# Batch 1's first softmax five steps later, and state's read with 32-column weights and a transpose

## The chip, the core and the metric

The kernel runs on one core of a Trainium2 chip. The metric is the device time of one execution in microseconds (us); the time before is the median of three runs. The profile is of one further execution of the same program, so its times are those of that one execution.

## The reference

The program computes an attention with a learned state of 32 rows for each head (4 batches, 8 heads, 512 positions, 64 columns a head), and sends the result, 4 x 544 rows of 512, through two feed-forward layers with 2048 inner columns. Cut to what matters here:

```python
scores  = scale * x @ state.T                  # B, H, 512, 32
a       = softmax(scores)                      # "first softmax", over the 32 state rows
xread   = a @ state                            # 512 rows a head
scores2 = scale * state @ x.T                  # B, H, 32, 512
a2      = softmax(scores2)                     # "second softmax", over the 512 positions
sread   = a2 @ x                               # "state's read", 32 rows a head
x1 = concat([xread, sread])                    # 544 rows a batch
h  = x1 @ w_in ;  g = h - tanh(h) ;  x2 = g @ w_out
h  = x2 @ w2_in;  g = h * tanh(softplus(h)) ;  out = g @ w2_out
```

Everything is float32. The attention's own products are plain float32; a feed-forward product is made of three products of a large and a small part (names ending in h and l, type fp32r).

## The kernel before

The first feed-forward layer runs as a list of steps, `seq`: 16 steps for each batch (a step is one tile of 128 inner columns for the 512 rows of a batch), 4 steps for the state rows of all batches after batch 2, and then batch 3. Batch 0 has steps 0 to 15, batch 1 steps 16 to 31, batch 2 steps 32 to 47, the state rows 48 to 51, batch 3 steps 52 to 67. Step i issues an "up" (six products into `h`, from `ath`, `atl`, `swh`, `swl`) and then the "down" of three steps before (twelve products into `acc`, from `gh`, `gl` and the weights). Between the two stand the side jobs of that step, entered with `at(step, ...)`: reading weights in and splitting them (`conv_w1o`, names `w`, `r`, `wh`, `wl`), products of a batch's state with weights (`sw`, names `swp`, `swh`, `swl`), and the attention of the next batches. A framework then orders the instructions of each engine, each engine runs its own in that order, and semaphores tie the engines together.

For one batch the attention is: transposes of x (`xt_t`, bank `xtp`), scores (`sc_m`, bank `sct`, copied to `scs`), for each half j the first softmax (`at_exp`: transpose into bank `sc`, maximum, subtraction, exponential; `at_norm`: sum, reciprocal, product, all on tile `a`), the second softmax (`at_exp_t`, on `scs`), its transpose (`at_read_t`, bank `e2p`, copied to `e2`), and state's read (`at_sread`, bank `srd`), which goes into `xst` for steps 48 to 51. `at_a` transposes `a` (bank `atp`) into `ath` and `atl`, which the batch's "up" steps read. VectorE (DVE) does reductions and differences, ScalarE (ACT) the exponentials, tanh and half of the copies. Beyond the start, all side jobs share two PSUM banks (`side_bank`), one after the other.

In `at_sread` a product has 64 columns of x as its weights and 32 columns of the softmax as what moves, and writes 64 partitions; two of them (i = 0 and 1) write the two halves of the partitions.

The profile gives line 63 for nearly every instruction (a helper issues them), so the rows are told apart by the tiles' names; a tile in a second kind of buffer is called `wide`.

Of the kernel before, what the change touches and what calls it, by code (L numbers as in the profile page):

```python
# [75 lines left out]
def attention_moe_kernel(  # L76
# [12 lines left out]
    NS = state.shape[2]  # L89
# [3 lines left out]
    KD = DM // 128  # L93
# [10 lines left out]
    TE, AC, V = (Pinned(e, order) for e in (nc.tensor, nc.scalar, nc.vector))  # L104
# [13 lines left out]
    def get(name, dtype=F32, newest=False):  # L118
        if halves and dtype == F32:
            return halves.popleft()  # L120
        i = free.pop() if newest else free.popleft()
        return Unit(slots.tile([128, 512], dtype, tag=f"k{i}", name=name), i)

    def put(*units):
        for u in units:
            if u.slot is None:
                halves.append(u)
            else:
                free.append(u.slot)
# [4 lines left out]
    def side_bank(name):  # L134
        ps_n[0] += 1
        return psum.tile([128, 512], F32, tag=banks[ps_n[0] % len(banks)], name=name)

    ident = misc.tile([128, 128], F32, name="ident")
# [271 lines left out]
    def load_x(b, ks=range(KD)):  # L410
        for k in ks:
            u = get("x", newest=b > 1)
            (nc.gpsimd if b > 1 else nc.sync).dma_start(
                out=u.t.rearrange("p (h c) -> p h c", h=2),
                in_=x[b, 2 * k:2 * k + 2].rearrange("h (p r) d -> p h (r d)", r=4),
            )
            X[b, k] = u

    def x_tile(b, k, i, r):
        c = i * 256 + r * 64  # L420
        return X[b, k].t[:, c:c + 64]

    P = {}
# [17 lines left out]
    def at_xt(b, k):  # L441
        xt_t(b, k)
        xt_c(b, k)
# [31 lines left out]
    def at_scores(b):  # L475
        sc_m(b)
        for j in range(2):
            sc_c(b, j)

    def sc_t(b, j):  # L480
        P["s", b, j] = ps = side_bank("sc")
        for r in range(4):
            TE.transpose(
                out=ps[:, r * 128:(r + 1) * 128],
                in_=SC[b, j].t[:, r * 128:(r + 1) * 128],
                identity=ident,
            )

    def sc_max(b, j):
        P["m", b, j] = mx = small.tile([128, 16], F32, tag="mx", name="mx")  # L490
        V.tensor_reduce(out=mx, in_=v3(P["s", b, j]), axis=AX.X, op=ALU.max)

    def sc_sub(b, j):
        A[b, j] = get("a")
        V.tensor_tensor(
            out=v3(A[b, j].t),
            in0=v3(P.pop(("s", b, j))),
            in1=P.pop(("m", b, j)).unsqueeze(2).to_broadcast([128, 16, NS]),
            op=ALU.subtract,
        )  # L500

    def sc_exp(b, j):
        AC.activation(out=A[b, j].t, in_=A[b, j].t, func=ACTF.Exp, scale=scale)

    def at_exp(b, j):
        sc_t(b, j)
        sc_max(b, j)
        sc_sub(b, j)
        sc_exp(b, j)

    def nm_sum(b, j):
        P["n", b, j] = sm = small.tile([128, 16], F32, tag="sm", name="sm")
        V.tensor_reduce(out=sm, in_=v3(A[b, j].t), axis=AX.X, op=ALU.add)

    def nm_rec(b, j):
        sm = P["n", b, j]
        V.tensor_scalar(out=sm, in0=sm, scalar1=1e-9, scalar2=None, op0=ALU.add)
        V.reciprocal(out=sm, in_=sm)

    def nm_mul(b, j):  # L520
        a3 = v3(A[b, j].t)
        V.tensor_tensor(
            out=a3,
            in0=a3,
            in1=P.pop(("n", b, j)).unsqueeze(2).to_broadcast([128, 16, NS]),
            op=ALU.mult,
        )

    def at_norm(b, j):
        nm_sum(b, j)  # L530
        nm_rec(b, j)
        nm_mul(b, j)

    def at_exp_t(b, j):
        e = SC.pop((b, j))
        mt = small.tile([128, 2], F32, tag="mt", name="mt")
        V.tensor_reduce(out=mt[:, 0:1], in_=e.t, axis=AX.X, op=ALU.max)
        V.tensor_scalar(
            out=mt[:, 0:1], in0=mt[:, 0:1], scalar1=-scale, scalar2=None, op0=ALU.mult
        )  # L540
        AC.activation(
            out=e.t, in_=e.t, func=ACTF.Exp, scale=scale, bias=mt[:, 0:1], accum_out=mt[:, 1:2]
        )
        V.tensor_scalar(
            out=mt[:, 1:2], in0=mt[:, 1:2], scalar1=1e-9, scalar2=None, op0=ALU.add
        )
        V.reciprocal(out=mt[:, 1:2], in_=mt[:, 1:2])
        V.tensor_scalar(
            out=e.t, in0=e.t, scalar1=mt[:, 1:2], scalar2=None, op0=ALU.mult
        )  # L550
        ET[b, j] = e

    def at_read_t(b, j):
        ps = side_bank("e2p")
        e = ET.pop((b, j))
        for r in range(4):
            TE.transpose(
                out=ps[:, r * 128:(r + 1) * 128],
                in_=e.t[:, r * 128:(r + 1) * 128],
                identity=ident,  # L560
            )
        u = get("e2")
        AC.activation(out=u.t, in_=ps, func=ACTF.Copy)
        put(e)
        ET[b, j] = u

    def at_sread(b):
        ps = side_bank("srd")
        u = [ET.pop((b, i)) for i in range(2)]
        for k in range(KD):  # L570
            for r in range(4):
                for i in range(2):
                    c = r * 128 + k * NS
                    TE.matmul(
                        out=ps[i * 64:(i + 1) * 64, k * NS:(k + 1) * NS],
                        lhsT=x_tile(b, k, i, r),
                        rhs=u[i].t[:, c:c + NS],
                        start=(r == 0),
                        stop=(r == 3),
                    )  # L580
        put(*u, *(X.pop((b, k)) for k in range(KD)))
        V.tensor_copy(
            out=xst[:, :, b * NS:(b + 1) * NS],
            in_=ps[:, :128].rearrange("p (k n) -> p k n", k=KD),
        )

    def at_steps(b):
        st = [lambda k=k: at_xt(b, k) for k in range(KD - 1)]
        return st + [
            lambda: at_xt(b, KD - 1),  # L590
            lambda: at_scores(b),
            lambda: (at_exp(b, 0), at_exp_t(b, 0)),
            lambda: at_norm(b, 0),
            lambda: (at_exp(b, 1), at_exp_t(b, 1), at_read_t(b, 0)),
            lambda: at_norm(b, 1),
            lambda: at_read_t(b, 1),
            lambda: at_sread(b),
        ]

    def at_a_hi(b, j):  # L600
# [469 lines left out]
    def at(step, fn, back=None):  # L1070

        def held():
            kept = [e.floor for e in engines]
            for e, m in zip(engines, marks[-back]):
                e.floor = m
            fn()
            for e, m in zip(engines, kept):
                e.floor = m

        side.setdefault(step, []).append(held if back else fn)  # L1080

    seq = []
    start = {}
# [14 lines left out]
        for c in range(4):  # L1098
            at(start[b] + 4 * c - 2, lambda b=b, c=c: sw(b, c))
    for j in range(2):  # L1100
        at(7 + j, lambda j=j: at_exp(1, j))
        at(8 + j, lambda j=j: at_norm(1, j))
        for b in range(2):
            k = start[1] + 4 + 2 * b + 4 * j
            at(k, lambda b=b, j=j: at_exp_t(b, j), 1)
            at(k + 3 - b, lambda b=b, j=j: at_read_t(b, j), 1)
            if j:
                at(k + 4 - b, lambda b=b: at_sread(b), 1)
    for b in (2, 3):
        at(start[b - 1], lambda b=b: load_x(b))  # L1110
        for i, f in zip((3, 4, 5, 7, 8, 9, 10, 11, 12, 13, 15), at_steps(b), strict=True):
            at(start[b - 1] + i, f)
    for b in (1, 2, 3):
        at(start[b] - (3 if b > 1 else 1), lambda b=b: at_a(b))
# [202 lines left out]
```

## Time and profile before

| | |
|---|---|
| median of 3 runs | 717.06 us (716.99 to 717.49) |
| the profiled execution | 717.59 us |
| its span, first to last instruction | 715.8 us |
| TensorE (PE) busy | 706.3 us |
| VectorE (DVE) busy | 464.7 us |
| ScalarE (ACT) busy | 352.5 us |
| granted TensorE clock | 1.0 throughout |

The span is 1.8 us shorter than the time of the same execution. A busy TensorE is a TensorE that has something in its pipe: its instructions overlap, so the distance from one start to the next says what one costs, not its duration. A float32 product stands in the trace as two records, each with its own weight load (PEld); a transpose and an fp32r product as one.

### The profile page before, as it was taken

What the parts mean: (1) busy time and instruction counts of PE and PEld (TensorE: products, weight loads), DVE (VectorE), ACT (ScalarE), POOL (GpSimd) and SP (SyncE); (2) the same over time, 40 slices, a digit from 0 to 9 for tenths busy, and PEclk for the clock granted to TensorE, in tenths of its full rate; (3) what the DMA queues carried; (4) which work ended last, traced back from release to release, by engine and by line L of the source; (5) the groups of instructions that cost most, each with busy time, mean ns of one, the idle gap of its engine ahead of it and who ended that gap; (6) DMA issues with size and microseconds to landing.
All of it is one profiled execution on the core that took longest, in us unless ns stands there. A gap on an engine that the chain in (4) does not pass through costs nothing.

```text
span 715.8 us, 10555 instructions
## 1 busy us (share of the span) xinstructions
PE 706.3 (99%) x3974; PEld 566.4 (79%) x3974; DVE 464.7 (65%) x793; ACT 352.5 (49%) x631; POOL 70.5 (10%) x110
## 2 busy tenths in 40 slices
PE   8899999999999999999999999999999999999998
PEld 6467777778777898777878888888888888888886
DVE  5899755675758747798647875557753455545654
ACT  6998545556765656867537342224333223222320
POOL 0000010022412224420304100000000000000000
PEclk9999999999999999999999999999999999999999
DMA  9985210124644357691978654445866244322003
GB/s 288 341 278 195 60 60 1 31 89 145 215 172 147 118 177 251 220 381 45 335 269 286 230 173 153 142 150 147 292 199 213 89 163 153 126 77 85 1 1 132
DMA packets 52643, 118.66 MB, mean 166 GB/s; under 512 B 7280, under 2 KB 11632, under 8 KB 52592
## 3 DMA queue, kind: packets, MB, share of 16 engines
q1 hardware_dynamic: 44272, 90.72, 38.4%
q0 software_dynamic: 8320, 27.27, 10.5%
q8 instruction: 31, 0.51, 0.3%
q14 instruction: 20, 0.16, 0.1%
HBM read 88.34 MB, written 29.62 MB: 165 GB/s over the span
## 4 chain that ended last, share of the span: by engine, by line
PE 87%; ACT 7%; DVE 4%; issue 1%; DMA 1%; SPq 0%
PE acc L63 48%; PE h L63 32%; ACT r L63 2%; ACT w L63 2%; PE swp L63 2%; PE hs L63 2%; PE srd L63 1%; ACT gh L63 1%; DMA x<-in_x_dram 1%; DVE w L63 1%; ACT t L63 1%; DVE wide L63 1%; PE xtp L63 1%; DVE a L63 1%; PE sct L63 1%
## 5 line engine op out<-in xcount | busy, mean ns | idle before, releaser
L63 PE MATMUL acc<-wo,gh 128*128 128x512 f32 (+1 forms) x548 | 168.1, 388 | 0.0
L63 PE MATMUL h<-yh,ws 128*128 128x512 f32 x448 | 156.7, 391 | 0.1
L63 PEld LDWEIGHTS acc<-wo,gh 128*128 128x128 f32 x548 | 102.1, 188 | 21.0 <-ACT gh L63 0.4
L63 DVE TENSOR_TENSOR wide<-acc,wide 128x512 f32<-128x512 f32 (+1 forms) x99 | 67.7, 684 | 74.5 <-PE acc L63 73.2
L63 PE MATMUL acc<-wo,gl 128*128 128x512 f32 (+1 forms) x274 | 106.3, 388 | 0.0
L63 PE MATMUL acc<-gh,wh 128*128 128x512 f32 x244 | 99.1, 406 | 0.0
L63 PEld LDWEIGHTS h<-yh,ws 128*128 128x128 f32 x448 | 84.1, 188 | 17.8 <-DVE mt L63 0.5
L63 PE MATMUL acc<-gh,wl 128*128 128x512 f32 x244 | 95.6, 392 | 0.0
L63 PE MATMUL acc<-gl,wh 128*128 128x512 f32 x244 | 95.1, 390 | 0.0
L63 PE MATMUL h<-yl,ws 128*128 128x512 f32 x224 | 87.2, 389 | 0.0
L63 DVE TENSOR_TENSOR gl<-wide,gh 128x512 fp32r<-128x512 f32 x70 | 48.3, 690 | 48.1 <-ACT gh L63 48.0
L63 DVE TENSOR_TENSOR wide<-h,wide 128x512 f32<-128x512 f32 x92 | 63.2, 687 | 21.6 <-ACT wide L63 10.4
L63 ACT ACTIVATE wide<-wide 128x512 f32<-128x512 f32 x47 | 29.7, 633 | 85.4 <-DVE wide L63 85.4
L63 ACT ACTIVATE wide<-h 128x512 f32<-128x512 f32 x39 | 23.3, 596 | 75.6 <-PE h L63 74.8
L63 PEld LDWEIGHTS acc<-wo,gl 128*128 128x128 f32 x274 | 51.5, 188 | 10.9 <-DVE gl L63 0.4
L63 PEld LDWEIGHTS acc<-gh,wh 128*128 128x128 f32 x244 | 45.8, 188 | 17.2 <-issue 5.6
L63 PEld LDWEIGHTS acc<-gh,wl 128*128 128x128 f32 x244 | 45.8, 188 | 11.3 <-issue 1.2
L63 PE MATMUL h<-ath,swh 128*128 128x512 f32 x128 | 51.8, 405 | 1.8 <-DVE t L63 1.0
L63 PEld LDWEIGHTS acc<-gl,wh 128*128 128x128 f32 x244 | 45.9, 188 | 8.5
L63 DVE TENSOR_TENSOR t<-h,t 128x512 f32<-128x512 f32 x54 | 36.9, 685 | 23.5 <-ACT t L63 23.4
L63 PE MATMUL h<-ath,swl 128*128 128x512 f32 x128 | 50.5, 395 | 0.5 <-DVE swl L63 0.5
L63 PE MATMUL h<-atl,swh 128*128 128x512 f32 x128 | 50.0, 390 | 0.0
(158 smaller groups left out, 1037.4 us busy)
## 6 DMA issues: line engine op xcount, KB each, us to landing
ws<-wi SPq DMA_DIRECT2D x128, 256.0 KB, 3.8
wo<-wo SPq DMA_DIRECT2D x64, 256.0 KB, 3.8
st<-in_moe_w_in_dram SPq DMA_DIRECT2D x27, 512.0 KB, 5.6
st<-in_moe_w_out_dram SPq DMA_DIRECT2D x22, 512.0 KB, 4.8
wi<-wh POOLq DMA_DIRECT2D x32, 256.0 KB, 4.1
wi<-wl POOLq DMA_DIRECT2D x32, 256.0 KB, 4.3
wide<-in_moe_w_out_dram SPq DMA_DIRECT2D x10, 512.0 KB, 5.3
wo<-wh POOLq DMA_DIRECT2D x16, 256.0 KB, 5.0
```

What stands on the lines that cost most here:

```text
L63: i = fn(*args, **kw)
```

## The change

Three things are changed. Batch 1's first softmax (`at_exp(1, j)` and `at_norm(1, j)`) stands at steps 12 to 14 and no longer at 7 to 9. State's read takes 32 columns of the softmax as weights and 64 columns of x as what moves, in the order i, r, k, so that four successive products write the four quarters of the partitions; the result goes to a tile `sr`, and a new job `at_sturn` two or more steps later turns it with one 128x128 transpose (bank `srt`) into `xst`. And batch 3's attention, with the load of its x, stands two or three steps earlier.

```diff
     def at_sread(b):
         ps = side_bank("srd")
         u = [ET.pop((b, i)) for i in range(2)]
-        for k in range(KD):
+        for i in range(2):
             for r in range(4):
-                for i in range(2):
+                for k in range(KD):
                     c = r * 128 + k * NS
                     TE.matmul(
-                        out=ps[i * 64:(i + 1) * 64, k * NS:(k + 1) * NS],
-                        lhsT=x_tile(b, k, i, r),
-                        rhs=u[i].t[:, c:c + NS],
+                        out=ps[k * NS:(k + 1) * NS, i * 64:(i + 1) * 64],
+                        lhsT=u[i].t[:, c:c + NS],
+                        rhs=x_tile(b, k, i, r),
                         start=(r == 0),
                         stop=(r == 3),
                     )
         put(*u, *(X.pop((b, k)) for k in range(KD)))
+        P["r", b] = o = get("sr")
+        V.tensor_copy(out=o.t[:, :128], in_=ps[:, :128])
+
+    def at_sturn(b):
+        ps = side_bank("srt")
+        u = P.pop(("r", b))
+        TE.transpose(out=ps[:, :128], in_=u.t[:, :128], identity=ident)
+        put(u)
         V.tensor_copy(
             out=xst[:, :, b * NS:(b + 1) * NS],
...
-        at(7 + j, lambda j=j: at_exp(1, j))
-        at(8 + j, lambda j=j: at_norm(1, j))
+        at(12 + j, lambda j=j: at_exp(1, j))
+        at(13 + j, lambda j=j: at_norm(1, j))
...
                 at(k + 4 - b, lambda b=b: at_sread(b), 1)
+                at(k + 7 - b, lambda b=b: at_sturn(b), 1)
+    when = {2: (3, 4, 5, 7, 8, 9, 10, 11, 12, 13, 15, 16), 3: (0, 1, 3, 4, 5, 7, 8, 9, 10, 11, 12, 13)}
     for b in (2, 3):
-        at(start[b - 1], lambda b=b: load_x(b))
-        for i, f in zip((3, 4, 5, 7, 8, 9, 10, 11, 12, 13, 15), at_steps(b), strict=True):
+        at(start[b - 1] - 2 * (b - 2), lambda b=b: load_x(b))
+        for i, f in zip(when[b], at_steps(b), strict=True):
             at(start[b - 1] + i, f)
```

**VectorE, steps 7 to 9.** The order of VectorE's instructions from the second half of step 6 on (`mx`, `sm` and `a` are the first softmax's, `w`, `wl` the weights', `t`, `gl` a step's own). Before:

```order
L63 TENSOR_TENSOR wl<-w,wh 128x512
L63 SCALAR_TENSOR_TENSOR w<-w,r 128x512 x2
L63 TENSOR_REDUCE mx<-sc 128x16
L63 TENSOR_TENSOR t<-h,t 128x512
L63 TENSOR_TENSOR a<-sc,mx 128x512
L63 TENSOR_TENSOR wl<-w,wh 128x512
L63 TENSOR_TENSOR gl<-t,gh 128x512
L63 SCALAR_TENSOR_TENSOR w<-w,r 128x512
L63 TENSOR_REDUCE sm<-a 128x16
```

Now:

```order
L63 TENSOR_TENSOR wl<-w,wh 128x512
L63 SCALAR_TENSOR_TENSOR w<-w,r 128x512 x3
L63 TENSOR_TENSOR t<-h,t 128x512
L63 TENSOR_TENSOR wl<-w,wh 128x512
L63 SCALAR_TENSOR_TENSOR w<-w,r 128x512
L63 TENSOR_TENSOR gl<-t,gh 128x512
```

The softmax's instructions are gone from between the weights' and the step's own, here and in the two steps that follow.

**VectorE, steps 12 to 14.** The same engine behind the second `swl` of step 11, up to the `swl` of step 14. Before:

```order
L63 TENSOR_TENSOR wl<-w,wh 128x512 x2
L63 TENSOR_TENSOR t<-h,t 128x512
L63 TENSOR_TENSOR gl<-t,gh 128x512
L63 TENSOR_TENSOR t<-h,t 128x512
L63 TENSOR_TENSOR gl<-t,gh 128x512
L63 SCALAR_TENSOR_TENSOR w<-w,r 128x512
L63 CAST wh<-w 128x512
```

Now:

```order
L63 TENSOR_TENSOR wl<-w,wh 128x512
L63 TENSOR_REDUCE mx<-sc 128x16
L63 TENSOR_TENSOR t<-h,t 128x512
L63 TENSOR_TENSOR a<-sc,mx 128x512
L63 TENSOR_TENSOR gl<-t,gh 128x512
L63 TENSOR_REDUCE sm<-a 128x16
L63 TENSOR_SCALAR sm<-sm 128x16
L63 RECIPROCAL sm<-sm 128x16
L63 TENSOR_TENSOR a<-a,sm 128x512
L63 TENSOR_REDUCE mx<-sc 128x16
L63 TENSOR_TENSOR t<-h,t 128x512
```

The softmax's instructions, six for each half, stand here now (the last ones shown begin the second half), ahead of the `swl` of step 14 and of the transposes of `a` at step 15.

**TensorE, step 29.** The order of TensorE behind batch 1's state read (`e2p` and `atp` are transposes, `acc` the twelve products of a "down"). Before:

```order
L63 MATMUL srd<-e_1504,x 64x32
L63 MATMUL srd<-wide,x 64x32
L63 MATMUL e2p<-ident,wide 128x128 x4
L63 MATMUL acc_1307<-gh,wh 128x512
L63 MATMUL acc_1307<-gl,wh 128x512
L63 MATMUL acc_1307<-gh,wl 128x512
L63 MATMUL atp<-ident,a 128x128 x8
L63 MATMUL acc_1308<-gh,wh 128x512
```

Now:

```order
L63 MATMUL srd<-x,e_1504 32x64 x16
L63 MATMUL srd<-x,e_1762 32x64 x16
L63 MATMUL e2p<-ident,wide 128x128 x4
L63 MATMUL atp<-ident,a 128x128 x4
L63 MATMUL acc_1307<-gh,wh 128x512
L63 MATMUL acc_1307<-gl,wh 128x512
L63 MATMUL acc_1307<-gh,wl 128x512
L63 MATMUL atp<-ident,a 128x128 x4
L63 MATMUL acc_1308<-gh,wh 128x512
```

Half of the transposes of `a` stand before the three products that were ahead of all eight. The four new transposes stand in three other places: one right before batch 2's read (step 31), two side by side at step 32, one at step 45.

## Rows read from the trace of the kernel before

**Rows 1.** The page: engines' busy time; the chain that ended last, by engine.

```profile
PE 706.3 (99%) x3974; PEld 566.4 (79%) x3974; DVE 464.7 (65%) x793; ACT 352.5 (49%) x631; POOL 70.5 (10%) x110
...
PE 87%; ACT 7%; DVE 4%; issue 1%; DMA 1%; SPq 0%
```

**Rows 2.** Windows: stretch, length, then each engine's busy time, clock, DMA share, GB/s.

```profile
48.00:69.20 21.20, 21.20 (x104) 17.22 (x96) 20.61 (x39) 19.60 (x36) 0.00 (x0) 1.00 0.67 241
69.20:75.40 6.20, 5.71 (x35) 3.51 (x35) 6.20 (x12) 4.65 (x9) 0.00 (x0) 1.00 0.00 0
75.40:89.00 13.60, 13.60 (x119) 10.90 (x118) 8.75 (x14) 6.34 (x11) 0.00 (x0) 1.00 0.26 78
...
177.00:252.00 75.00, 75.00 (x460) 58.78 (x459) 53.44 (x99) 48.16 (x88) 19.99 (x30) 1.00 0.48 162
...
363.00:716.00 353.00, 349.23 (x1594) 289.83 (x1593) 204.65 (x320) 114.80 (x196) 9.12 (x14) 1.00 0.46 151
```

**Rows 3.** Timeline of PE at step 12: start, duration, idle time before and its releaser.

```profile
73.17 0.50 PE L63 MATMUL h<-ath,swh 128*128 128x512 f32 x1
...
74.39 0.50 PE L63 MATMUL h<-ath,swl 128*128 128x512 f32 x1 [0.49 <-DVE swl L63]
```

**Rows 4.** Timeline of DVE at steps 7 and 12.

```profile
53.18 0.68 DVE L63 TENSOR_REDUCE mx<-sc 128x16 f32<-128x512 f32 x1
53.78 0.68 DVE L63 TENSOR_TENSOR t<-h,t 128x512 f32<-128x512 f32 x1
...
73.66 0.68 DVE L63 TENSOR_TENSOR swl<-swp,swh 128x512 fp32r<-128x512 f32 x1
```

**Rows 5.** Timeline of PE at step 29: first, second and last pairs of batch 1's read.

```profile
160.44 0.24 PE L63 MATMUL srd<-e,x 128*64 128x32 f32 x1
...
160.52 0.22 PE L63 MATMUL srd<-e,x 128*64 128x32 f32 x1
160.53 0.22 PE L63 MATMUL srd<-wide,x 128*64 128x32 f32 x1
...
162.27 0.22 PE L63 MATMUL srd<-e,x 128*64 128x32 f32 x1
```

**Rows 6.** The chain in order of time, 153 to 176 us: start, length, what.

```profile
173.49 1.99 PE srd L63 x64
```

**Rows 7.** Timeline of PE at step 24: batch 2's scores, 256 columns on 32-column tiles.

```profile
133.48 0.38 PE L63 MATMUL sct<-wide,sbt 64*32 64x256 f32 x1
...
133.52 0.38 PE L63 MATMUL sct<-wide,sx 64*32 64x256 f32 x1
133.69 0.38 PE L63 MATMUL sct<-wide,sbt 64*32 64x256 f32 x1
```

**Rows 8.** Timeline of PE in the second layer: two transposes between products.

```profile
525.47 0.39 PE L63 MATMUL acc<-wo,gl 128*128 128x512 f32 x1
525.70 0.38 PE L63 MATMUL gt<-ident,wide 128*128 128x128 f32 x2
...
526.15 0.40 PE L63 MATMUL h<-yl,ws 128*128 128x512 f32 x1
```

**Rows 9.** Timeline of ACT at step 29.

```profile
160.55 0.60 ACT L63 ACTIVATE t<-h 128x512 f32<-128x512 f32 x1 [2.06 <-PE h L63]
...
161.90 0.63 ACT L63 ACTIVATE gh<-t 128x512 fp32r<-128x512 f32 x1
...
163.18 0.60 ACT L63 ACTIVATE wide<-e2p 128x512 f32<-128x512 f32 x1 [0.65 <-PE e2p L63]
```

**Rows 10.** Timeline of DVE at step 29.

```profile
161.18 0.69 DVE L63 TENSOR_TENSOR t<-h,t 128x512 f32<-128x512 f32 x1 [2.45 <-ACT t L63]
...
162.54 0.29 DVE L63 COPY xst<-srd 128x128 f32<-128x128 f32 x1
```

**Rows 11.** Timeline of POOL, whose queue issues stores and batch 3's x.

```profile
179.36 0.72 POOL L261 DMA_DIRECT2D wi<-wh  x1 [12.74 <-ACT wh L63]
```

**Rows 12.** Tile x, 85 to 260 us, POOL's part: last line of the answer.

```profile
DMA to landing us min/median/max: 3.1/3.3/4.3
```

More of the change, by code (lines that the diff above doesn't have):

```diff
@@ L597, in at_steps @@
             lambda: at_sread(b),
+            lambda: at_sturn(b),
         ]
```

## The prediction

> **What bounds the kernel now.** I read the page first, then windows, then timelines of the places that the change touches. The page has TensorE busy for 706.3 of 715.8 us, and the chain that ended last is TensorE's for 87% [rows 1]. So the question is which stretches leave TensorE waiting. The windows answer it [rows 2]: from 177 to 252 us, where batch 3's attention lies, it is busy for 75.00 of 75.00; after 363 us it lacks 3.8 us in 353, in the second layer and the tail, where the change has no instruction. From 48 to 69 us TensorE is full too, but VectorE is busy for 20.61 and ScalarE for 19.60 of 21.20: weights are being read in. From 69.2 to 75.4 VectorE is never idle and TensorE lacks 0.5 us. That is the one wait near the moved softmax: at step 12 the third product of the "up" starts 1.22 us after the first [rows 3], where two ordinary distances of 0.23 (525.47 to 525.70 [rows 8]) make 0.46. It is 0.76 late, and its releaser is `swl`, which VectorE began at 73.66 and held for 0.68 [rows 4]: the product starts 0.05 after it. VectorE was behind with its queue.
>
> Where TensorE is full, a microsecond taken from its instructions is one taken from the end, as long as nothing that it waits for becomes the last; where it waits for VectorE, only VectorE's work counts.
>
> **The change part by part.** The sum is made against the profiled execution, 717.59 us.
>
> *State's read.* The old read runs in pairs: i = 0 and i = 1 start 0.01 apart [rows 5], so two halves of the columns work at once. From the second pair to the last, 160.52 to 162.27, are 30 distances: 58.3 ns a pair. 32 pairs (16 products for each i, two records each) make 1.87, and with 0.12 for getting in and out that is the 1.99 of [rows 6]. The new read has the same 64 records. If its four quarters work at once, they are 16 rounds. No row shows 128 rows by 32 columns, so a round's price is bounded. From below: in the scores, on tiles of 32 columns by 64 rows, eight records start within 0.04 and the same tile starts again 0.21 later with 256 columns moving [rows 7]; 64 columns need a quarter, 53 ns. From above: weights and stream might lie one behind the other, half of 58.3 for half the weight columns and 53 for the stream, 82 ns. I take 58.3, the row of the same operation with the same 128 rows: its 128 weight columns for a pair are again 128 for a round of four. So 16 rounds go, 0.93 us a read, 3.73 for four (bounds 2.24 and 4.08). A read is then 1.05 long.
>
> The Trainium skill ("TensorE: Matmul & The Clock Gate", section on LDWEIGHTS) has a weight load take its columns over 1.2 GHz, 53 ns for 64 and 27 for 32. By that the old pair would be bound by weights and the new round by its stream, and this term 4.08; the rows here cannot separate the two, since both give the old pitch.
>
> *The turns.* Four transposes are added. Two between products push the second product behind them from 0.46 to 0.68 us after the last one ahead (525.47 to 526.15 [rows 8]): 0.22. They stand in three places. Two single ones cost between 0.11 and 0.22 each, 0.13 taken since little of it is entry; the two at step 32 cost 0.22. Together 0.48. The four extra copies on VectorE (0.29 each [rows 10]) lie beside TensorE's work: VectorE has 21 us free between 177 and 252 [rows 2].
>
> *The split of `atp` at step 29.* One more entry to transposes, 0.05 (0 to 0.1).
>
> *A new wait at step 29.* Two banks serve all side jobs. The read uses one, `e2p` the other, the first half of `atp` the first again, the second half the second. So the first half waits for VectorE's copy of `srd`, the second for ScalarE's copy of `e2p`. I count from the start of the read, 160.44 [rows 5], which I call E. ScalarE starts tanh at E + 0.11 and `gh` at E + 1.46 [rows 9]; VectorE starts `t` at E + 0.74 [rows 10], and a large instruction holds it for 0.60 (53.18 to 53.78 [rows 4]). In the new order the copy of `srd` follows `t`: E + 1.34 to 1.63. TensorE, a microsecond sooner, is through with the read and `e2p` (four transposes, 0.43) at E + 1.48: 0.15 of waiting. Behind that come four transposes and three products, to E + 2.8; but ScalarE's copy of `e2p` now stands behind `gh` and a `wh`, some 0.6 each, and is done at about E + 3.2. That is 0.4 more. 0.6 in all (0 to 1.2: nothing if ScalarE gets there sooner, double if a weight is late). Queued behind it on TensorE is the rest of the "down" and all later work, so it counts in full. Before, the copy of `e2p` started at 163.18, E + 2.74, and nothing waited.
>
> *The softmax five steps later.* VectorE loses from steps 7 to 9 eight large instructions of 0.60 and four small ones, about 5.2 us, in a stretch where it was full to the end; that is more than the 0.76 by which `swl` was late. So that wait goes: -0.76 (bound 0). The transposes `sc` cost TensorE the same in either place. The work comes back at steps 12 to 14, where VectorE is busy for 8.75 of 13.60 [rows 2], part of it the backlog that is gone by then. With 5.2 more it is nearly full, but the last product on `a` is needed only at step 15. I take no new wait, and price one below.
>
> *Batch 3 three steps earlier.* Same instructions; TensorE is full in the old place and in the new. Its x is issued at step 30 by POOL's queue and first read at step 32; a load lands 3.3 us after its issue [rows 12], and two steps of 18 products at 0.23 are 8.3. Taken as 0.
>
> The sum: -3.73 + 0.48 + 0.05 + 0.60 - 0.76 = -3.36, so 714.23 for the profiled execution. The median stands 0.53 below it (717.06), so I forecast **713.7**. What a measurement of this kernel can tell from no change is about 0.2%, 1.4 us; the forecast is beyond it.
>
> **The rivals.**
>
> *Weights do not overlap with the stream.* Rounds of 82 ns, a term of 2.24, and a wait at step 29 of 0.2 since TensorE comes later: -2.24 + 0.53 + 0.2 - 0.76 = -2.27, 714.8. For it: no row shows four quarters with all 128 rows, and 58.3 is also what half weights and half stream in series could give. Against it: in the pairs the records already lie on one another, 0.22 long and 0.058 apart. The Trainium skill (same page, Part 3, "The mechanism") says that a weight load overlaps with running matmuls only where the row group differs; here all have all rows, so by that rule this rival would hold. Chance 0.12.
>
> *The quarters do not run four abreast.* Two abreast, as now: the reads stay at 1.99, the wait at step 29 does not arise, and -0.76 + 0.53 leaves 716.8, no change. One at a time: 64 x 58.3 = 3.73 and the 0.12, so 7.5 more over four reads, 724.3. Against both: the scores run on four column quarters (and two row halves) at once [rows 7]. Chances 0.05 and 0.03.
>
> *VectorE is late at steps 12 to 15.* 8.75 + 5.2 is 13.95 in 13.60 us if the backlog is not gone in time; then `atp` at step 15 or the "up" of step 16 waits, between 1 and the 2.6 us that one half of the softmax costs VectorE: 714.7 to 716.3. It decides from the moment when the last product on `a` ends after TensorE reaches step 15. For it: VectorE runs in order, and its softmax alternates with ScalarE's exponential. Against it: from the transposes of step 13 it has two steps, 8.3 us, for four instructions of the softmax and some six of the steps' own, 6 us. Chance 0.08.
>
> *Slower: batch 3's x comes late.* POOL runs its queue in order, and the last of the four loads, which the first transpose needs, stands behind four stores of weights. Before the change a store stood for 12.74 us until ScalarE had its `wh`, and was issued at 179.36 [rows 11]. If those four are late like it, the first goes out at about 177.3 (2 us of TensorE's time are saved by then), the load after four of 0.72 at 180.2, and it lands at 183.5. TensorE reaches the transpose 57 products at 0.23 (13.1 us) and some 5 us of side jobs, two reads among them, after the start of step 29's read, which is now 160.44 - 0.76 - 0.93 = 158.75: at about 177. It would wait 6.5 us: 720.2. It decides from an issue later than about 173.7. Against it: the stores ahead of the load are others, of weights that are split before step 30. Chance 0.06.
>
> **How the numbers follow.** The forecast has 0.66, the rivals 0.12, 0.05, 0.03, 0.08 and 0.06. The range: below, the stream's bound of a round (0.35 less) and no wait at step 29 (0.60 less), 712.7, and 0.2 for cheaper turns; above, rounds of 82 ns with the double wait (714.8 + 1.0), and half of the lateness at step 15: 712.5 to 716.3. It leaves out x late, the quarters two or one abreast and little else, some 0.16. Faster by over 0.2% (below 715.6) is the forecast, the first rival and half of VectorE late: 0.82. No change: two abreast and the other half, 0.09. Slower: 0.09.
>
> **What would show it.** In the profile after, `srd` should start its rounds 58 ns apart, four within 0.03 us, and take 1.05 in the chain. TensorE's wait for `swl` at step 12 should be gone, and VectorE idle at times before 73 us. At step 29 `atp` should wait for VectorE's `sr` and for ScalarE's `e2`, 0.6 together. `xtp` of batch 3 should wait for no DMA. Wrong would be the forecast if rounds are 80 ns or the records one after another, if `atp` at step 15 waits for `a`, or if ScalarE's waits for stores, which now hold other buffers, reach TensorE between 177 and 215 us.

## The result, and the profile after

The changed kernel takes **721.03 us** (median of 4, 720.63 to 721.57), the kernel before in the same session 717.02: a ratio of 1.0056, interval 1.0039 to 1.0074. It is slower, where 713.7 was forecast. The profiled execution took 720.96 us, its span is 719.2.

The page of the changed kernel: busy time, and the chain by engine and by line.

```profile
PE 705.6 (98%) x3978; PEld 564.6 (79%) x3978; DVE 466.9 (65%) x797; ACT 351.2 (49%) x631; POOL 70.5 (10%) x110
...
PE 76%; issue 8%; ACT 6%; POOL 4%; DVE 2%; DMA 2%; SPq 1%; POOLq 0%; ACTq 0%; DVEq 0%
PE acc L63 43%; PE h L63 28%; POOL wi L261 3%; PE hs L63 2%; ACT r L63 2%; PE swp L63 1%; ACT w L63 1%; DMA x<-in_x_dram 1%; ACT t L63 1%; DMA wi<-wl 1%; ACT gh L63 1%; PE xtp L63 1%; DMA wi<-wh 1%; POOL wo L261 1%; PE sct L63 1%
```

Against [rows 1], TensorE's share of the chain fell from 87 to 76%, and POOL's stores (`wi`) and their landings (DMA) are new in it. So what ends last now runs through the stores of split weights. The windows say where; the first three answer to [rows 2], the last two are the place.

```profile
69.20:75.40 6.20, 6.20 (x37) 5.07 (x30) 5.31 (x10) 3.86 (x7) 0.00 (x0) 1.00 0.27 82
75.40:89.00 13.60, 13.60 (x126) 11.07 (x125) 11.95 (x23) 7.38 (x13) 0.00 (x0) 1.00 0.13 42
177.00:252.00 75.00, 70.93 (x438) 54.43 (x437) 50.87 (x97) 44.78 (x82) 19.53 (x29) 0.98 0.48 167
...
188.00:194.00 6.00, 3.35 (x15) 2.43 (x13) 1.38 (x3) 2.39 (x5) 0.00 (x0) 1.00 0.27 89
194.00:200.00 6.00, 4.58 (x15) 3.50 (x16) 5.07 (x8) 4.70 (x9) 0.00 (x0) 0.72 0.24 74
```

At steps 12 to 15 everything went as forecast: TensorE is full. But between 177 and 252 us, where it had been busy for 75.00 of 75.00, it now lacks 4.07, all of it between 188 and 200. TensorE's timeline there (step 35):

```profile
190.96 0.39 PE L63 MATMUL h<-ath,swl 128*128 128x512 f32 x1
195.25 1.03 PE L63 MATMUL xtp<-ident,x 128*128 128x128 f32 x4 [3.91 <-DVE swl L63]
196.45 0.79 PE L63 MATMUL acc<-gh,wh 128*128 128x512 f32 x1 [0.16 <-DVE y L63]
197.04 0.63 PE L63 MATMUL acc<-gl,wh 128*128 128x512 f32 x1
197.47 0.63 PE L63 MATMUL acc<-gh,wl 128*128 128x512 f32 x1
...
198.75 0.43 PE L63 MATMUL acc<-gh,wl 128*128 128x512 f32 x1
199.01 0.40 PE L63 MATMUL acc<-gh,wh 128*128 128x512 f32 x1
```

It stands 3.91 us for `swl`, and then runs four distances between products, 197.04 to 198.75, at 0.43, about half the clock. To see who is late, go back from `swl` (194.51 on VectorE) over `gl`, ScalarE's `gh` and VectorE's `t` to ScalarE's `t`. ScalarE's timeline:

```profile
176.69 0.60 ACT L63 ACTIVATE t<-h 128x512 f32<-128x512 f32 x1 [1.46 <-PE h L63]
180.66 0.66 ACT L63 ACTIVATE r<-st 128x512 uint32<-128x512 uint32 x1 [3.37 <-DMA wi<-wh]
...
181.71 0.63 ACT L63 ACTIVATE gh<-t 128x512 fp32r<-128x512 f32 x1
...
183.63 0.61 ACT L63 ACTIVATE wh<-s 128x512 fp32r<-128x512 f32 x1
...
185.68 0.63 ACT L63 ACTIVATE gh<-t 128x512 fp32r<-128x512 f32 x1 [0.47 <-DVE t L63]
191.34 0.66 ACT L63 ACTIVATE r<-st 128x512 uint32<-128x512 uint32 x1 [5.03 <-DMA wi<-wh]
191.90 0.58 ACT L63 ACTIVATE t<-h 128x512 f32<-128x512 f32 x1
```

Two instructions `r` of conversions, which belong to steps 36 and 37 by the written order, stand ahead of the steps' own `t` and `gh`. Each writes a buffer from which a store has yet to read, so it waits for that store to land: 3.37 us, then 5.03. And the stores wait for ScalarE's `wh`, which stand behind the first `r`. POOL's timeline:

```profile
177.05 0.73 POOL L261 DMA_DIRECT2D wi<-wl  x1 [0.79 <-DVE wl L63]
183.15 0.73 POOL L261 DMA_DIRECT2D wi<-wh  x1 [5.38 <-ACT wh L63]
...
186.84 0.72 POOL L261 DMA_DIRECT2D wi<-wl  x1
```

The first `r` holds back three `wh`, these hold back six stores, and the second `r` waits for one of them. The step's own `t` behind it waits for a store too: in the chain of the changed kernel the last of the six lands right ahead of it.

```profile
186.84 5.04 DMA wi<-wl
191.88 0.02 issue
191.90 0.59 ACT t L63
```

So the late stores alone would have held `t` to 191.88; that the second `r` by itself cost anything is not shown. It is the first `r`, ahead of the `wh`, that makes the stores late. What it does to those behind it shows in `gh` at 181.71: VectorE had the `t` that it reads ready at 178.08.

```profile
177.40 0.68 DVE L63 TENSOR_TENSOR t<-h,t 128x512 f32<-128x512 f32 x1
```

The Trainium skill ("Perfetto Trace Analysis", section on the TensorE instruction) calls the queues of ScalarE and VectorE strictly first in, first out. This trace agrees: that `gh` began 3.6 us after its input was there, behind the `r`.

### The profile page after: what moved, and what is told of

It is laid out like the page before. It is cut to its first block, busy times and chain, and to the rows that moved or that the text cites. A ratio compares the mean times of both kernels' runs of the same rounds, so it can differ in the third digit from the quotient of the medians.

```text
span 719.2 us, 10576 instructions
## 1 busy us (share of the span) xinstructions
PE 705.6 (98%) x3978; PEld 564.6 (79%) x3978; DVE 466.9 (65%) x797; ACT 351.2 (49%) x631; POOL 70.5 (10%) x110
## 4 chain that ended last, share of the span: by engine, by line
PE 76%; issue 8%; ACT 6%; POOL 4%; DVE 2%; DMA 2%; SPq 1%; POOLq 0%; ACTq 0%; DVEq 0%
PE acc L63 43%; PE h L63 28%; POOL wi L261 3%; PE hs L63 2%; ACT r L63 2%; PE swp L63 1%; ACT w L63 1%; DMA x<-in_x_dram 1%; ACT t L63 1%; DMA wi<-wl 1%; ACT gh L63 1%; PE xtp L63 1%; DMA wi<-wh 1%; POOL wo L261 1%; PE sct L63 1%
## 5 line engine op out<-in xcount | busy, mean ns | idle before, releaser
L63 DVE TENSOR_TENSOR wide<-acc,wide 128x512 f32<-128x512 f32 (+1 forms) x85 | 58.1, 683 | 64.3 <-PE acc L63 63.0
L63 DVE TENSOR_TENSOR wide<-h,wide 128x512 f32<-128x512 f32 x98 | 67.4, 688 | 27.7 <-ACT wide L63 13.8
L63 DVE TENSOR_TENSOR gl<-wide,gh 128x512 fp32r<-128x512 f32 x76 | 52.5, 691 | 49.7 <-ACT gh L63 48.7
L63 ACT ACTIVATE wide<-h 128x512 f32<-128x512 f32 x45 | 26.8, 594 | 81.7 <-PE h L63 79.5
L63 ACT ACTIVATE gh<-wide 128x512 fp32r<-128x512 f32 x76 | 48.0, 631 | 9.9 <-DVE wide L63 8.0
```

The costliest lines, as they stand in the source:

```text
L63: i = fn(*args, **kw)
```

## The experiments

Theory S: buffers of stored weights are handed out too early, since batch 3's x is taken at step 30. Theory Q: batch 3's own instructions are in the way. Theory T: TensorE is early and the background work does not follow. Later M, L, B and H, each told where it comes in.

To follow a kernel through its steps I compare the start of the weights' product `swp` on TensorE with the kernel before, from both timelines (us, minus is earlier). The moved instructions of batch 3 alone shift it by 1 to 2 us between steps 34 and 50.

| step | 30 | 34 | 38 | 42 | 50 | 54 | 58 | 62 |
|---|---|---|---|---|---|---|---|---|
| changed kernel | -2.3 | -1.9 | +4.8 | +4.0 | +2.3 | +2.3 | +3.9 | +3.5 |
| b3_back | -2.0 | -2.5 | -1.8 | -1.8 | -2.7 | +2.5 | +2.9 | +2.7 |
| hold9 | -3.2 | -2.8 | -2.0 | -2.8 | -4.5 | -2.4 | -1.4 | +1.9 |
| b3_only | -0.1 | +0.8 | +1.6 | +0.8 | -0.1 | -0.1 | +1.5 | +1.0 |
| reads_only | -1.1 | -1.7 | -1.1 | -1.1 | -1.9 | +3.7 | +4.4 | +4.1 |
| after_pin_35_37 | -2.1 | -1.7 | -0.9 | -1.8 | -3.5 | -3.5 | -1.9 | -2.3 |
| after_pin1 | -2.4 | -2.1 | -1.3 | -2.1 | -3.8 | -3.8 | -3.8 | -4.3 |

**b3_back, load_early: batch 3 back, wholly or but for its load.** The last two lines are b3_back's alone. In both, batch 3's read stands at step 46, one step ahead of its place in the kernel before, and its turn at 47.

```diff
-    when = {2: (...), 3: (0, 1, 3, 4, 5, 7, 8, 9, 10, 11, 12, 13)}
+    when = {2: (...), 3: (3, 4, 5, 7, 8, 9, 10, 11, 12, 13, 14, 15)}
-        at(start[b - 1] - 2 * (b - 2), lambda b=b: load_x(b))
+        at(start[b - 1], lambda b=b: load_x(b))
```

> The changed kernel with batch 3's x loaded at step 32 and its attention at steps 35 to 47, as before the change; the reads, the turns and batch 1's softmax stay changed. Theory S (slots): the stall of about 6 us at 189 to 200 us in the changed kernel is ScalarE's queue standing for stores of split weights whose buffers were handed out again too early, because batch 3's four x buffers are taken at step 30, before batch 2's are given back; with the load back at step 32 the stall goes and the time is the predicted sum, 713.5 to 714.5 us. Theory Q (order): batch 3's own instructions, three steps earlier, stand in ScalarE's and VectorE's queues ahead of the work that TensorE waits for; it expects the same 713.5 to 714.5. Theory T (earlier TensorE): the reads and the removed stall brought TensorE forward by 2 to 3 us and the stores did not follow; the stall stays, 719 to 721 us.

> The changed kernel with only batch 3's attention put back to steps 35 to 47; its x is still loaded at step 30. Theory S, with the early taking of the four buffers as the cause, expects the stall to stay: 717 to 721 us, with a wait of ScalarE for a store of several us between 176 and 200 us. Theory Q expects it gone: 713.5 to 714.5 us. Theory T expects 719 to 721 us.

Measured: 720.59 us (1.0049, 1.0037 to 1.0062) and 720.32 (1.0043, 1.0031 to 1.0056). The stall at steps 34 to 36 is gone in both, and one of 5 to 6 us stands between steps 50 and 54 instead. S and Q, which make batch 3 the cause of the loss, fall; only that the first stall goes with batch 3's attention put back is as Q has it.

**hold9: stored buffers given back later.**

```diff
-HOLD = 6
+HOLD = 9
```

> The changed kernel with HOLD 9 in place of 6: a stored buffer is given back three counts later, so nothing takes it within three steps of its store. Theory S expects the stall gone and the time that of the predicted sum, 713 to 715.5 us. Theory Q expects the stall to stay, since batch 3's instructions stand where they stood: 719.5 to 721.5 us. Theory T, too, expects it to go.

Measured: 718.78 us (1.0026, 1.0013 to 1.0039). The stall at 34 to 36 goes, as S and T have it, and 6.4 us are lost in three pieces behind step 50. So the early hand-out is not the cause of the loss. That it had a part in the first stall is not shown by this run alone, since ScalarE's order is another here too.

**b3_only: batch 3 earlier, and nothing else.** The edit is the change's last hunk, with the old reads.

> The kernel before with batch 3's x loaded at step 30 and its attention at steps 32 to 44, and nothing else changed. Theories S and Q expect the stall here too: 717.0 plus 4 to 6.5, that is 721 to 723.5 us. Theory T expects no stall, 716.3 to 717.7 us, since TensorE is not earlier here.

Measured: 718.97 us (1.0030, 1.0017 to 1.0043), missed by all three. TensorE is not early here and yet loses 1.6 us between steps 54 and 58, 1.3 of them in a wait for ScalarE's `ys`.

**reads_only, softmax_only: the other two parts alone.** The edits are the diff's hunks on `at_sread` and `at_sturn` (the turn at step 32 for batch 2, as in the changed kernel, and at 47 for batch 3, with its read at 46), and the two lines on `at_exp` and `at_norm`.

> The kernel before with the new reads and turns for all four batches, and nothing else changed (batch 1's softmax at steps 7 to 9, batch 3 at steps 35 to 47). In the runs so far TensorE reaches step 48 between 2.7 and 4.5 us early, as the sum has it, and loses 5 to 7 us at one later place, another one in each kernel. Theory T (TensorE early, the background conversions and their transfers do not follow, and the queues of ScalarE and VectorE stand in their written order): a loss here too, since the reads alone bring TensorE 2 us or more forward, 717 to 721 us. Theory M (batch 3's move and the softmax's move, not the reads, bring the loss): the terms of the reads and turns alone, 717.0 less 3.7 and plus 0.5 to 1.0, 713.8 to 714.5 us.

> The kernel before with batch 1's first softmax at steps 12 to 14 and nothing else changed. The term of the sum is 0.76 us: 716.0 to 716.5 us if TensorE keeps what it gains at step 12. Theory T expects that 1 us is too little to run into the background work: 716 to 717 us. Theory M expects a loss of its own only if ScalarE's and VectorE's order later is another: 717 us or more.

Measured: reads_only **721.70 us** (1.0063, 1.0050 to 1.0077), softmax_only **716.20** (0.9987, 0.9978 to 0.9996). So M falls, T's 721 is missed by 0.7, and the part that should bring most loses most, by itself. Of reads_only, ScalarE's timeline at step 50, and TensorE's:

```profile
271.78 0.66 ACT L63 ACTIVATE w<-st 128x512 f32<-128x512 f32 x1 [2.49 <-DMA st<-in_moe_w_in_dram]
272.34 0.62 ACT L63 ACTIVATE gh<-wide 128x512 fp32r<-128x512 f32 x1
...
281.18 0.47 PE L63 MATMUL acc<-wh,gh 128*128 128x512 f32 x1 [3.69 <-DVE wide L63]
```

It is another place and another transfer (a load of raw weights), but the same pattern: a conversion waits 2.49 us for a DMA, and the `gh` that a step needs stands behind it. How much of TensorE's 3.69 us these 2.49 make is not shown: its wait begins some 5 us behind that `gh` and ends on a copy of VectorE. One thing sets softmax_only apart: 621 of ScalarE's 631 instructions stand there in the sequence of the kernel before (the longest sequence that both traces have in common, by the tiles' names without buffer numbers). In reads_only it is 550, in the changed kernel 504.

**after_nobg, before_nobg: no background work in steps 24 to 67.**

```diff
-    pace = [(start[1] + 8, 0), (start["s"], 52), (start["2"], 96)]
+    pace = []
```

> The changed kernel with the background conversions of the second weights taken out of steps 24 to 67 and all done behind step 67. The whole time says little; read from it is when TensorE begins its step 67, against the same edit of the kernel before. Theories T and S expect that without the background work the sum of the prediction shows there: 3 to 4.5 us earlier than in the other, with no wait of TensorE over 1.5 us between steps 24 and 67. Theory Q (batch 3's own instructions stand in the way) expects the stall at steps 34 to 36 to stay: 1 to 4 us later.

> The kernel before with the same edit: the background conversions behind step 67. It is what the kernel named after_nobg is compared with, by the moment at which TensorE begins step 67. Theories S and T expect it to stand 3 to 4.5 us behind that kernel; theory Q 1 to 4 us ahead.

Measured, one execution each: 822.70 and 825.78 us, 3.08 less with the change. At step 62, the last with a `swp`, the changed one is 3.12 us ahead (the sum of the prediction is 3.36), and the list of TensorE's waits between 125 and 340 us is empty in both. So the sum of the terms is there, but for 0.2 us, when no conversion is in the queues.

**reads_own, reads_own2, b3_back_own: a buffer of its own for the read's result.** Theory L is T under a sharper name (a lead that the background can't follow). Theory B: `sr` takes one of six half tiles that `t` and `y` use first. (H is told at the next runs.) The lines are those of reads_own and b3_back_own.

```diff
-        P["r", b] = o = get("sr")
-        V.tensor_copy(out=o.t[:, :128], in_=ps[:, :128])
+        V.tensor_copy(out=sr, in_=ps[:, :128])
```

> The kernel reads_only with one more edit: the read's result goes to a small buffer of its own instead of one taken from the shared buffers, where it took one of the six half tiles that t, y and the conversions take first. Buffers are then handed out at steps 28 to 46 as in the kernel before. Theory B (buffers): the taken half moves t, y and the conversions of the steps behind it to other buffers, those to wait for other releases, and ScalarE's and VectorE's queues get another order; without that the terms of the reads and turns show, 713.8 to 714.8 us. Theory L (lead: TensorE 2 us early and the background does not follow, whatever the buffers): 719.5 to 722 us, with a stall of 4 us or more between 180 and 300 us.

> The kernel reads_own with a buffer of two halves, one for even and one for odd batches, so that no batch's read overwrites another's (in reads_own and b3_back_own batch 1's read overwrites batch 0's, and part of the output is another). Theories H and B expect no difference to reads_own, 716.9 to 718.3 us: its losses are a wait for ScalarE's ys of 2.1 us and one at about 310 us, behind the reads.

> The kernel b3_back (reads, turns, batch 1's softmax later, batch 3 as before) with the read's result in a small buffer of its own. Theory B expects the sum of the gains that the runs so far show, 717.1 less 0.9 (softmax_only) and less 2.3 to 3.3: 713 to 714 us. Theory L: 719 to 721 us.

Measured: 717.60 us (1.0001, 0.9992 to 1.0009), 717.62 (1.0001, 0.9993 to 1.0010) and 716.72 (0.9990, 0.9981 to 0.9998). For reads_own and b3_back_own both theories miss: 4 us of the loss are gone, but the gain isn't there; reads_own2 comes out as reads_own. TensorE is still up to 2.8 us ahead at step 54 in reads_own, and then waits for `ys` 2.1 us.

**after_pin1, before_pin1: a rule for the order.** Theory H: conversions hoisted ahead of a step's own work are the cause.

```diff
+                        kept = [e.floor for e in engines]
+                        AC.floor, V.floor = marks[-1][1:]
                         run_piece()
+                        for e, m in zip(engines, kept):
+                            e.floor = m
```

> The changed kernel with one more rule for the order on ScalarE and VectorE: an instruction of the background conversions of step i does not stand ahead of the last instruction written in step i-1. Theory H (an instruction of a conversion stands ahead of work that TensorE waits for, and itself waits for a transfer): the stall at steps 34 to 36 goes or shrinks to under 2 us, 713.5 to 717 us. Theory L: the conversions come later still, and the time stays at 719 to 722 us. Theory B: buffers are handed out as in the changed kernel, so the stall stays or moves, 718 to 722 us.

> The kernel before with the same rule for the order. It shows what the rule is worth by itself. Theories H, B and L expect about no change, 716 to 718 us, since TensorE waits for no conversion in the kernel before behind step 24.

Measured: after_pin1 **713.23 us** (0.9940, 0.9927 to 0.9954), before_pin1 717.91 (1.0006, 0.9997 to 1.0016). The rule alone is worth nothing; with it the change is worth 0.6%. Windows of after_pin1, and the longest waits of its TensorE behind the start (sum, times, longest):

```profile
177.00:252.00 75.00, 75.00 (x470) 58.58 (x470) 53.39 (x100) 47.51 (x87) 20.98 (x31) 1.00 0.51 172
252.00:330.00 78.00, 78.00 (x501) 64.01 (x500) 62.75 (x103) 55.04 (x100) 20.35 (x32) 1.00 0.63 210
```

```profile
PE h L63 <- DVE t L63: 1.0, 1, 1.0
PE xtp L63 <- DMA x<-in_x_dram: 1.0, 3, 0.5
PE h L63 <- ACT swh L63: 0.8, 1, 0.8
```

All of these lie in the first 125 us.

In the list of ScalarE's waits between 100 and 340 us no DMA is left; the changed kernel has four there, 8.4 us of `r` for `wi<-wh` the largest. L falls: TensorE is 4 us ahead and the background follows. ScalarE's order is not that of the kernel before again: 508 of its 631 instructions stand in that sequence, about as few as in the changed kernel. So the number of re-sorted instructions does not tell a loss; which of them stand ahead of a step's work does.

**after_pin_35_37: the rule at three steps alone.** The diff is the same with `if 35 <= i <= 37`. Rows of ScalarE's order of the changed kernel, and then of this one (DMASW is the wait for a store):

```
219 L63 ACTIVATE t_2055<-h_2048 128x512 [waits PE_49]
220 L63 ACTIVATE r_2290<-st_1133 128x512 [waits DMAHW7_49,DMASW0_49,DVE_49]
221 L63 ACTIVATE wide_72<-xtp_2068 128x512 [waits PE_49]
...
228 L63 ACTIVATE gh_2113<-t_2110 128x512 [waits DVE_49]
229 L63 ACTIVATE r_2352<-st_1551 128x512 [waits DMAHW0_49,DMASW6_49,Activation_49]
230 L63 ACTIVATE t_2161<-h_2154 128x512 [waits DMASW7_49,PE_49]

219 L63 ACTIVATE t_2055<-h_2048 128x512 [waits PE_49]
220 L63 ACTIVATE wide_72<-xtp_2068 128x512 [waits PE_49]
...
227 L63 ACTIVATE gh_2113<-t_2110 128x512 [waits DVE_49]
228 L63 ACTIVATE t_2161<-h_2154 128x512 [waits DMASW7_49,PE_49]
...
239 L63 ACTIVATE r_2290<-st_1133 128x512 [waits DMAHW7_49,DMASW0_49]
...
245 L63 ACTIVATE r_2352<-st_1551 128x512 [waits DMASW6_49]
```

> The changed kernel with the rule of after_pin1 at steps 35 to 37 alone. On ScalarE that moves the conversion's r, which waits for a store of split weights, from ahead of step 34's t to behind step 37's; buffers, stores and all waits for them stay as in the changed kernel. Theory H: the stall at 189 to 200 us goes, the one of 1.3 us at about 302 us may stay: 714 to 716.5 us. Theory B (the buffers are the cause, the order is not): the stall stays, 719 to 721.5 us.

Measured: 715.18 us (0.9980, 0.9968 to 0.9992). The same buffers and the same stores; the two `r` stand 19 and 16 places later, the second behind step 36's `t` (not step 37's, as I had it). ScalarE's timeline, POOL's first delayed store, and TensorE:

```profile
186.25 0.60 ACT L63 ACTIVATE t<-h 128x512 f32<-128x512 f32 x1 [2.58 <-PE h L63]
...
193.65 1.23 ACT L63 ACTIVATE r<-st 128x512 uint32<-128x512 uint32 x2
...
197.39 0.66 ACT L63 ACTIVATE r<-st 128x512 uint32<-128x512 uint32 x1
...
180.16 0.73 POOL L261 DMA_DIRECT2D wi<-wh  x1 [2.20 <-ACT wh L63]
...
191.17 0.39 PE L63 MATMUL h<-ath,swl 128*128 128x512 f32 x1
191.40 0.60 PE L63 MATMUL xtp<-ident,x 128*128 128x128 f32 x4
...
193.22 0.39 PE L63 MATMUL acc<-gh,wh 128*128 128x512 f32 x1
```

`t` starts 5.65 us earlier and waits for TensorE, not for a store; the store leaves 3 us earlier, and both `r` (the second of the pair at 193.65, and the one at 197.39) wait for nothing. Up to the place of the stall these two are all that moved on ScalarE, and `t_2161` keeps its wait for a store (DMASW7); the store is now there in time. The loss of 1.3 us for `ys` stays, as H has it. So with the same buffers the order decides whether this stall is there, and B, as its sole cause, falls. The runs do not part the first `r` from the second, nor do they show what other buffers would do in the old order.

**reads_only_pin1, b3_back_pin1: the terms without the stall.**

> The kernel reads_only, which took 721.7 us, with the rule for the order at all steps. Theory H: the reads' and turns' terms alone, 717.3 less 3.7 and plus 0.5 to 1.0, so 714.1 to 714.8 us. Theory L (TensorE early by the reads, the background does not follow): 719 us or more.

> The kernel b3_back, which took 720.6 us, with the rule for the order at all steps. Against after_pin1 it shows what batch 3's three steps are worth without a stall in ScalarE's queue. The prediction's term is 0, so by theory H 712.9 to 713.8 us, as after_pin1 (713.23); by theory L 719 us or more.

Measured: 714.55 us (0.9962, 0.9950 to 0.9973) and 713.25 (0.9942, 0.9929 to 0.9955), both as H has it.

## Why the prediction was wrong, point by point

*The reads*: right. The chain has 1.03 us for one (below); 1.05 was forecast, 1.99 before [rows 6]. In the changed kernel's last read, where one of the four column quarters reads its x from a `wide` tile, the rounds can be told apart: six from 240.68 to 241.02, 0.057 each, and four records within 0.03 us, as forecast.

```profile
240.68 0.22 PE L63 MATMUL srd<-wide,e 128*32 128x64 f32 x1
240.69 0.23 PE L63 MATMUL srd<-x,e 128*32 128x64 f32 x3
240.74 0.22 PE L63 MATMUL srd<-wide,e 128*32 128x64 f32 x1
...
241.02 0.22 PE L63 MATMUL srd<-wide,e 128*32 128x64 f32 x1
```

reads_only_pin1 stands 2.78 us below its kernel before; -3.73 + 0.48 + 0.05 + 0.60 is -2.60.

*The turns*: right. The chain of after_pin1 shows a read, a single turn and the pair; 0.13 and 0.22 were forecast.

```profile
152.77 1.03 PE srd L63 x64
...
171.07 0.11 PE srt L63
...
176.53 0.22 PE srt L63 x2
```

*The split of `atp` and the wait at step 29*: right. In the changed kernel `e2p` (timeline of TensorE) holds 0.65 up to `atp`, where 0.43 was counted, and the three products before the second half hold 1.06, against three ordinary distances of 0.23: 0.22 and 0.37 together 0.59, which contains the entry from transposes to products.

```profile
159.56 0.66 PE L63 MATMUL e2p<-ident,wide 128*128 128x128 f32 x4
160.21 0.66 PE L63 MATMUL atp<-ident,a 128*128 128x128 f32 x4
160.62 0.48 PE L63 MATMUL acc<-gh,wh 128*128 128x512 f32 x1
...
161.68 0.66 PE L63 MATMUL atp<-ident,a 128*128 128x128 f32 x4
```

*The softmax*: right. softmax_only gains about 0.9 us (ratio 0.9987), 0.76 was forecast. TensorE is busy for 6.20 of 6.20 us around step 12, so the wait of [rows 3] is gone, and the rival "VectorE is late" did not come: VectorE is busy for 11.95 of 13.60 there.

*Batch 3*: as a price, right: b3_back_pin1 and after_pin1 differ by 0.02 us. The rival "x late" did not come: between 100 and 340 us TensorE waits for no DMA in the changed kernel. But by itself and without the rule it costs 1.8 us (b3_only).

**The step that failed** is the premise under the sum, with the order of the other instructions as a term of nothing: "a microsecond taken from its instructions is one taken from the end, as long as nothing that it waits for becomes the last". The working applies it at each edited place, to the buffers and banks that the edit uses, and takes the order of ScalarE's other instructions for given. It is not: some 80 (reads_only) to 130 (the changed kernel) of its 631 instructions left their sequence, conversions of weights went ahead of steps' own work and of the `wh` that stores wait for, and the waits for stores and loads reached TensorE. The last sentence of the prediction names just that ("ScalarE's waits for stores, which now hold other buffers, reach TensorE between 177 and 215 us"), but it stands in no rival, with no price and no chance. It was the outcome: about 6 us at steps 34 to 36 and 1.3 in a wait for `ys` between steps 54 and 58, against gains that, with the order held, come to 4.1 us (3.36 were forecast; what makes the difference was not separated).

What stays open: which of the edits' side effects moves which instruction. A private buffer restored part of the order (576 of 631, by the count above) and 4 us of the time in reads_own2, so the buffer is one of them; the others were not separated. That the `ys` wait is of the same kind is argued from after_pin1, where the rule at all steps removes it; it was not followed to its start.

## What to carry to other kernels

Where an in-order engine carries both a step's own work and background work that waits for transfers, an edit's effect on the order of that queue is a term of the sum, with a price: the longest wait for a DMA that the trace shows on that engine, put in front of the work that the bound engine needs. Here that price would have been too low: the longest such wait of ScalarE between 100 and 340 us of the kernel before is 2.9 us, and about 6 were lost in the first stall, since the delay held back the stores that later work waits for. So it is a lower bound, and it was not tried on another change. Look at such waits in the kernel before even when they cost nothing there. Then look in the new order for instructions that wait for a DMA and come from a later step than those behind them. If a change loses for no reason of its own, hold the order first and measure again before giving the change up.

That longest wait of the kernel before (sum, times, longest):

```profile
ACT r L63 <- DMA st<-in_moe_w_in_dram: 2.9, 1, 2.9
```

## What the runs showed of the hardware

- 64 records of 128 rows by 32 columns take 1.03 us, 16 ns each. The Trainium skill ("TensorE: Matmul & The Clock Gate", Part 3, "The mechanism") lets a weight load overlap with running matmuls only where the row group differs; all records here have all rows, and by rounds one after another the prediction had 82 ns a round, 1.3 us. The measurement decides: rounds 0.057 us apart, so four column quarters run at once.
- This wait of TensorE cost more than itself. After 3.91 us without work the granted clock of 194 to 200 us is 0.72, and four distances between products are 0.43 instead of 0.23, the lower of the two levels (1.2 GHz). From the four transposes to the seventh product behind them it takes 3.76 us (195.25 to 199.01), in after_pin_35_37 1.82 (191.40 to 193.22): another 1.9 us, 0.16 of it a wait for VectorE's `y`.
- Six stores of 256 KB issued one behind the other, as the two kernels have them, landed as follows, in the changed kernel and in after_pin_35_37 (the stores' line in 180 to 195 and 178 to 190 us):

```profile
DMA to landing us min/median/max: 2.6/3.1/5.1
...
DMA to landing us min/median/max: 2.6/3.1/3.4
```

The 5.04 us in the chain of the changed kernel are those of the sixth. To stand behind five others does not explain them, since the same six took 3.4 at most in the other kernel; why the last was late is not shown.
